# Routing products ahead of a second layer, weights' low parts later, and other places for the streamed tiles, in an attention and mixture-of-experts kernel

## The chip, the cores and the metric

The kernel runs on one core of a Trainium2 chip. The metric is the time of one execution on the device, in microseconds (us); it is the median of several runs. The engines are TensorE (PE in the rows; PEld is its weight load), VectorE (DVE), ScalarE (ACT), GpSimd (POOL) and SyncE (SP), which issues most of the DMAs.

## The reference

The first half is attention without a softmax: for each of 8 batches and 8 heads, the 64x64 product of keys and values over 576 positions is applied to the queries, and each row of 64 is divided by its root mean square and multiplied by g_norm. The second half sends each of the 4608 tokens (512 features) through one of 16 experts:

```
kv = np.einsum('bhsd,bhse->bhde', k, v)
out = np.einsum('bhsd,bhde->bhse', q, kv)
out = out / np.sqrt(np.mean(out * out, axis=-1, keepdims=True) + 1e-06) * g_norm
...
g_logits = x @ w_group                      # the group of 4 with the largest logit
e_logits = xg @ w_expert[g]                 # in it, the expert of 4 with the largest logit
h = np.maximum(xg[mask_e] @ w1[g, e], 0.0)  # 512 -> 1024
ye = h @ w2[g, e]                           # 1024 -> 512
out[tok_idx] = combined[:, None] * ye       # combined: the two softmax weights
```

## The kernel before

**Attention and routing (0 to about 128 us).** The 36 blocks of 128 tokens form six groups (`GS`). For each group the kernel computes the attention rows, stores them in a table in HBM (`scr`), and routes them: logits, the expert of each token, and its rank among the tokens of that expert. Which instruction stands where is decided by a planner: each piece of work is a `step` with an engine, an assumed duration, a rank and the steps it needs, and `give_out` hands them out in order of assumed time and rank. While the last groups are still routed, the expert that has most tokens early (the early expert, region 0) is already computed for 256 tokens: `early_products`, with float32 weights (`wr`), first layer into `h`, second layer into `l2` (`l_...` in the order's rows).

**The last routing products.** At the end, `slots` (one matmul per block) places the token numbers by expert and rank; `slt` is their sum so far. `eps` gives the experts' order by size, and from it `eidx`, the list of experts that the weight loads need. `gps` gives the token numbers of each expert in that order; VectorE turns it into the indices `gall`, which the gathers on POOL's queue need.

**The hand-over (about 128 to 159 us).** The early expert's second 128 tokens pass the second layer (`left`, two halves; `CUT` chunks of the second half run before the transposes of the third block's rows `xs`, the rest behind them). Its third block (`xr`, scaled to `xs`) then passes both layers in float32. Beside this the first streamed region is prepared: gather its rows (`xg`), scale them, store them to HBM (`xd`), load them back as `xq`, transpose them on VectorE (`xt`), split them into a high and a low part (`xh`, `xl`), and split the expert's weights in the same way (`whi`, `wlo`, by ScalarE and VectorE).

**The streamed regions (159 to 558 us).** The 15 other experts follow in order of size. Region r has `CAPS[r]` columns, one per token. Every product is a sum of three streamed matmuls in a reduced float32 format (fp32r): high x high, low x high and high x low. In the first layer each of 8 hidden chunks takes 4 x 3 matmuls (`ps`), in the second each of 4 output chunks 8 x 3 (`psy`): 192 matmuls of `CAPS[r]` columns a region. The weights are the stationary operand, the tokens (`xh`, `xl`, then `hh`, `hl`) are streamed. In the last region the second layer turns this round. While a region is computed, the next one is gathered, loaded, transposed and split, and its weights are loaded and split.

**Where tiles lie.** A pool gives tiles their places one behind the other. In the built program the weights (`w8`) begin at byte 27,008 of a partition plus whole multiples of 8,192, `xh` at 180,704, and `xl`, `hh`, `hl` whole multiples of 512 bytes behind `xh`; the float32 rows `xT` begin at 125,312 and `hT` at 127,360. A chunk of a streamed tile is 384 columns of 4 bytes, 1,536 bytes, so all chunks have the same place modulo 512.

Of the kernel before, what the change touches and what calls it, by code (L numbers as in the profile page):

```python
# [9 lines left out]
F32 = mybir.dt.float32  # L10
F32R = mybir.dt.float32r
# [3 lines left out]
ALU = mybir.AluOpType  # L15
# [5 lines left out]

CAPS = [384, 364, 354, 330, 326, 312, 302, 300, 292, 290, 284, 274, 268, 264, 260, 256]

# [30 lines left out]
MOVED = list(range(1, 15))  # L54
CUT = 5

@with_exitstack
def tile_linattn_moe(ctx: ExitStack, tc: tile.TileContext, qm, qt, k, v, router, w1, w2, out):
    nc = tc.nc
    P = 128  # L60
    B, H, S, D = BATCH, HEADS, SEQ, HEAD_DIM
# [15 lines left out]
    KC = DM // P  # L77
# [12 lines left out]
    ovt = tc.dram_tile([NBLK, 4], F32, name="ovt")  # L90

    cp = ctx.enter_context(tc.tile_pool(name="cp", bufs=1))
    big = ctx.enter_context(tc.tile_pool(name="big", bufs=BIG))

# [147 lines left out]

    def split_piece(w, p, turned=False):
        for x, hi, lo in quarter(w, p, turned):
            nc.scalar.copy(out=hi, in_=x)  # L245
            nc.vector.tensor_tensor(out=lo, in0=x, in1=hi.bitcast(F32), op=ALU.subtract)  # L246

# [88 lines left out]
    with ExitStack() as ph:  # L336
# [92 lines left out]
        def get(*key):  # L429
            return done.get(key)  # L430
# [199 lines left out]
        def route(g):  # L630
# [175 lines left out]
            def f():  # L806
                eng.tensor_tensor(
                    out=tl([1, NE, 6], "slot", BF16, bufs=1), in0=v["oh3"].unsqueeze(3).to_broadcast([P, nt, NE, 6]),
                    in1=v["jv"].rearrange("p t a j -> p t (a j)").unsqueeze(2).to_broadcast([P, nt, NE, 6]),
                    op=ALU.mult)  # L810
            sj = do(e, nt * 96, [sj, get("slots", g - 1)], f)

# [111 lines left out]
            if last:  # L924
                def f():
                    v["eps"] = ps_k.tile([P, 512], F32, name="eps", tag="psk")
                    nc.tensor.matmul(v["eps"][0:2, 0:3 * NE], lhsT=evec[0:NS, :], rhs=v["pmx"][0:NS, :], start=True,
                                     stop=True)
                x = do("PE", 0, [perm, done["ek", B - 1]], f, us=0.05)

                def f():
                    nc.vector.tensor_copy(out=eidx, in_=v["eps"][0:1, 0:3 * NE].rearrange("p (r j) -> p r j", j=3)[
                        :, :, 0])
                x = do("D", 16, [x], f)


                def f():
                    v["gps"] = ps_r.tile([P, 512], F32, name="gps", tag="psr")
                    nc.tensor.matmul(v["gps"][:, 0:3 * NE], lhsT=st["slt"][0:NS, :], rhs=v["pmx"][0:NS, :], start=True,
                                     stop=True)  # L940
                s = do("PE", 0, [s, x], f, us=0.1)

                def f():
                    nc.vector.tensor_scalar(out=gall[:, 0:3 * NE], in0=v["gps"][:, 0:3 * NE],
                                            scalar1=-1.0, scalar2=float(DUMMY), op0=ALU.mult, op1=ALU.add)
                done["gidx_last"] = do("D", 48, [s], f)
# [123 lines left out]
        def early_products(wt):  # L1070
# [34 lines left out]
            for j in range(1):  # L1105
                for hf in range(2):
                    def f(j=j, hf=hf):
                        t["l2", j, hf] = ps_e.tile([P, 512], F32, name="l2", tag="pse")
                        whole2(t["l2", j, hf][:, 0:DM // 2], t["h"][:, :, j * P:(j + 1) * P], st["ws"][2 + hf])
                    s = step("PE", 3.5, r0 + RANK["l2"] + 0.1 * (2 * j + hf), [free.pop(0), wt[2 + hf]] + hs, f)  # L1110

# [25 lines left out]
    with ExitStack() as ph:  # L1137
# [92 lines left out]
        def gather(r):  # L1230
            xg = mp.tile([P, 3, RW], F32, name="xg", bufs=1)
            for j, _ in blocks(CAPS[r]):
                st["gather"] = gather_rows(xg[:, j], P, gidx[:, r, j:j + 1])
            return xg
# [20 lines left out]

        def parts_x():
            return [mp.tile([P, KC, 384], F32R, name=nm, bufs=1) for nm in ("xh", "xl")]

# [70 lines left out]
        w1n, w2n, load_next = weight_loads(eidx[0:1, 1:2], mp)  # L1329
        for i in range(2):  # L1330
            load_next(i)
        nxt = gather(1)
# [11 lines left out]
        for p in range(2):  # L1344
            split_piece(w1n, p)
        keep_left(0)
        for j, _ in blocks(CAPS[1]):
            scale_rows(nc.vector, nxt[:, j])
        put_x(1, nxt)
        scale_rows(nc.vector, xr, xs)  # L1350
        xq, xt = get_x(1)
        for i in range(2, 4):
# [8 lines left out]
        scatter_rows(st["ys"][:, 1, :], P, gidx0[:, 1:2])  # L1361
        for p in range(2, 4):
            split_piece(w1n, p)

        for hf in range(2):
# [3 lines left out]
            nc.scalar.activation(out=hT[:, 4 * hf:4 * hf + 4], in_=ps.rearrange("p (f t) -> p f t", f=4), func=AF.Relu)  # L1369
        cur = parts_x()  # L1370
        for c in range(KC):
            turn_x(1, xq, xt, c)
        for c in range(KC):
            split_x(1, cur, xt, c)
        yo = mp.tile([P, DM], F32, name="yo", bufs=2)
        for hf in range(2):
# [13 lines left out]
        for r in range(1, NE):  # L1390
            cap = CAPS[r]
            xh, xl = cur
            hh = mp.tile([P, FC, 384], F32R, name="hh", bufs=1)
            hl = mp.tile([P, FC, 384], F32R, name="hl", tag="hl", bufs=1)
            if nxt:
# [32 lines left out]
            nw1a, nw2a, load_a = weight_loads(eidx[0:1, r + 2:r + 3], mp if r % 2 else None) if nxt2 else (None, None, None)  # L1428
            cur = parts_x() if nxt else None

# [139 lines left out]
```

## Time and profile before

| | us |
|---|---|
| runs: median (lowest to highest of 3) | 567.9 (567.41 to 568.88) |
| the profiled execution | 565.66 |
| its span, first to last instruction | 564.0 |
| TensorE busy | 543.9 |
| first streamed matmul / end of the last region's | 158.58 / 557.65 |

All rows are of the one profiled execution. The time of the profiled execution is its span and 1.66 us around it. Matmuls overlap: each is listed with a duration of about 300 ns, but the next one starts after 120 to 170 ns, so the spacing of their starts is what counts, not their durations. A float32 matmul appears as two entries in the counts. "issue" in the chain of waits is time in which the engine waited for nothing that the profile shows.

### The profile page before, as it was taken

What the parts mean: (1) busy time and instruction counts of PE and PEld (TensorE: products, weight loads), DVE (VectorE), ACT (ScalarE), POOL (GpSimd) and SP (SyncE); (2) the same over time, 40 slices, a digit from 0 to 9 for tenths busy, and PEclk for the clock granted to TensorE, in tenths of its full rate; (3) what the DMA queues carried; (4) which work ended last, traced back from release to release, by engine and by line L of the source; (5) the groups of instructions that cost most, each with busy time, mean ns of one, the idle gap of its engine ahead of it and who ended that gap; (6) DMA issues with size and microseconds to landing.
All of it is one profiled execution on the core that took longest, in us unless ns stands there. A gap on an engine that the chain in (4) does not pass through costs nothing.

```text
span 564.0 us, 11522 instructions
## 1 busy us (share of the span) xinstructions
PE 543.9 (96%) x4323; PEld 522.6 (93%) x4323; DVE 378.1 (67%) x782; ACT 267.1 (47%) x530; POOL 209.3 (37%) x278
## 2 busy tenths in 40 slices
PE   8999978699899999999999999999999999999995
PEld 3899868588899999999999999999999999999995
DVE  4247888773456796776767676777767686868750
ACT  0377754622444443544444544454546455546540
POOL 5024342144352342533453524344525334433121
PEclk9999998899999999999999999999999999999998
DMA  8999999486889999999998999999999999989940
GB/s 286 388 407 388 370 355 405 126 316 229 281 318 299 283 311 261 274 307 283 309 293 288 281 291 261 320 278 332 313 300 294 292 309 315 319 254 331 271 144 34
DMA packets 78890, 165.21 MB, mean 293 GB/s; under 512 B 8084, under 2 KB 47332, under 8 KB 67824
## 3 DMA queue, kind: packets, MB, share of 16 engines
q1 hardware_dynamic: 70862, 142.29, 78.7%
q0 software_dynamic: 7824, 22.11, 13.1%
q8 instruction: 35, 0.57, 0.4%
q10 hardware_dynamic: 146, 0.04, 0.1%
q14 instruction: 23, 0.19, 0.1%
HBM read 126.38 MB, written 38.55 MB: 292 GB/s over the span
## 4 chain that ended last, share of the span: by engine, by line
PE 69%; DMA 19%; issue 5%; DVE 2%; SPq 2%; ACT 2%; POOL 1%; POOLq 0%; DVEq 0%; ACTq 0%
PE ps L311 8%; PE ps L315 8%; PE ps L310 8%; DMA wr<-in_w_dram 8%; PE psy L311 8%; PE psy L310 8%; PE psy L315 8%; PE ops L515 5%; PE kps L477 3%; PE l L299 3%; PE warm L371 3%; DMA yd<-yq 2%; DMA xd<-xg 2%; DMA xq<-xd 2%; DMA ktail<-in_k_dram 2%
## 5 line engine op out<-in xcount | busy, mean ns | idle before, releaser
L246 DVE TENSOR_TENSOR wlo<-wr,whi 128x1024 fp32r<-128x1024 f32 (+1 forms) x176 | 156.6, 917 | 22.6 <-ACT whi L245 19.1
L311 PE MATMUL ps<-xl,whi 128*128 128x364 f32 (+14 forms) x480 | 144.5, 301 | 0.0
L315 PE MATMUL ps<-xh,wlo 128*128 128x364 f32 (+14 forms) x480 | 144.4, 301 | 0.0
L310 PE MATMUL ps<-xh,whi 128*128 128x364 f32 (+14 forms) x480 | 144.4, 301 | 0.0
L311 PE MATMUL psy<-hl,whi 128*128 128x364 f32 (+13 forms) x448 | 135.5, 302 | 0.0
L315 PE MATMUL psy<-hh,wlo 128*128 128x364 f32 (+13 forms) x448 | 135.4, 302 | 0.0
L310 PE MATMUL psy<-hh,whi 128*128 128x364 f32 (+13 forms) x448 | 135.2, 302 | 0.0
L245 ACT CAST whi<-wr 128x1024 fp32r<-128x1024 f32 (+1 forms) x176 | 128.2, 769 | 1.9 <-DMA wr<-in_w_dram 1.9
L284 ACT ACTIVATE hh<-ps 128x364 fp32r<-128x364 f32 (+14 forms) x120 | 50.4, 420 | 146.8 <-PE ps L315 142.4
L285 DVE SCALAR_TENSOR_TENSOR hl<-ps,hh 128x364 fp32r<-128x364 f32 (+14 forms) x120 | 55.8, 465 | 56.9 <-ACT hh L284 55.2
L310 PEld LDWEIGHTS ps<-xh,whi 128*128 128x128 f32 x480 | 90.8, 189 | 0.0
L315 PEld LDWEIGHTS ps<-xh,wlo 128*128 128x128 f32 x480 | 90.7, 189 | 0.0
L311 PEld LDWEIGHTS ps<-xl,whi 128*128 128x128 f32 x480 | 90.5, 189 | 0.0
L252 POOL DMA_INDIRECT xg<-scr,gall x44 | 52.6, 1196 | 96.2 <-DMA xd<-xg 81.2
L280 POOL TENSOR_TENSOR xg<-xg 128x256 f32<-128x256 f32 x82 | 60.2, 762 | 74.5 <-DMA xg<-scr,gall 74.4
L256 POOL DMA_INDIRECT out_dram<-yo,gall x45 | 51.8, 1150 | 92.8 <-DMA yo<-yd 75.9
L310 PEld LDWEIGHTS psy<-hh,whi 128*128 128x128 f32 x448 | 84.7, 189 | 0.0
L315 PEld LDWEIGHTS psy<-hh,wlo 128*128 128x128 f32 x448 | 84.7, 189 | 0.0
L311 PEld LDWEIGHTS psy<-hl,whi 128*128 128x128 f32 x448 | 84.5, 189 | 0.0
L1262 ACT ACTIVATE xh<-xt,rw 128x364 fp32r<-128x364 f32 (+14 forms) x60 | 32.3, 543 | 48.5 <-DVE xt L1253 45.5
L1315 DVE STREAM_TRANSPOSE yq<-psy 128x320 f32<-128x320 f32 (+3 forms) x56 | 28.5, 510 | 29.9 <-PE psy L315 27.6
L515 PE MATMUL ops<-kvx,m_q 128*128 128x168 f32 x256 | 42.0, 312 | 0.6 <-ACT xr L466 0.6
(250 smaller groups left out, 588.7 us busy)
## 6 DMA issues: line engine op xcount, KB each, us to landing
wr<-in_w_dram SPq DMA_DIRECT2D x64, 1024.0 KB
scr<-xo SPq DMA_DIRECT2D x36, 256.0 KB
m_q<-in_qm_dram SPq DMA_DIRECT2D x8, 1024.0 KB
xd<-xg SPq DMA_DIRECT2D x32, 256.0 KB
m_k<-in_k_dram SPq DMA_DIRECT2D x7, 1024.0 KB
m_v<-in_v_dram SPq DMA_DIRECT2D x7, 1024.0 KB
yo<-yd SPq DMA_DIRECT2D x28, 256.0 KB
xq<-xd SPq DMA_DIRECT2D x20, 160.0 KB
```

Source lines behind the costliest of these rows:

```text
L245: nc.scalar.copy(out=hi, in_=x)
L246: nc.vector.tensor_tensor(out=lo, in0=x, in1=hi.bitcast(F32), op=ALU.subtract)
L252: return nc.gpsimd.indirect_dma_start(out=xg[0:rows, 0:RW], out_offset=None, in_=src, in_offset=bass.IndirectOffsetOnAxis(ap=idx[0:rows, : ...
L256: sc = nc.gpsimd.indirect_dma_start(out=out, out_offset=bass.IndirectOffsetOnAxis(ap=idx[0:rows, :], axis=0), in_=yo[0:rows, :], in_offset ...
L280: d = eng.tensor_tensor(out=out_[:, hs], in0=x[:, hs], in1=factors(xg)[:, h], op=ALU.mult)
L284: nc.scalar.activation(out=hh, in_=ps, func=AF.Relu)
L285: nc.vector.scalar_tensor_tensor(out=hl, in0=ps, scalar=0.0, in1=hh.bitcast(F32), op0=ALU.max, op1=ALU.subtract)
L310: nc.tensor.matmul(ps, lhsT=stat_h(c), rhs=mov_h(c), start=(c == 0), stop=False)
L311: nc.tensor.matmul(ps, lhsT=stat_h(c), rhs=mov_l(c), start=False, stop=False)
L315: nc.tensor.matmul(ps, lhsT=stat_l(d), rhs=mov_h(d), start=False, stop=(d == n - 1))
L515: nc.tensor.matmul(o, lhsT=raw["q", b].rearrange("p j f -> p (j f)")[:, (pr * NJ + j) * P:(pr * NJ + j + 1) * P], rhs=kvx[b % 4][:, pr], s ...
L1262: nc.scalar.activation(out=xh, in_=x, func=AF.Copy, scale=g2[:, 0:1])
```

## The change

1. The second layer of the early expert (`l2`) now needs the step `done["last"]`, the last routing product `gps`; the planner can no longer put half of it ahead.
2. In the last group the product `slot` is computed on VectorE and no more on POOL.
3. The first streamed region's weights: the second half is loaded behind the stores of `xd`; the low parts of the first half are computed behind the scaling of the rows, and the second half is split behind `xh` and `xl`. `CUT` is 4 and no more 5.
4. Two regions get more columns: 326 becomes 330, 290 becomes 292.
5. Places: an unused tile of 8 floats ahead of all others moves everything by 32 bytes; `xg` is 24 floats (96 bytes) longer, so all that lies behind it, the streamed tiles among it, moves by 128 bytes; and a table `BEGIN` lets a region's streamed tiles begin at column 0, 8, 16 or 40 of the 384.

```
-CAPS = [384, 364, 354, 330, 326, 312, 302, 300, 292, 290, 284, 274, 268, 264, 260, 256]
+CAPS = [384, 364, 354, 330, 330, 312, 302, 300, 292, 292, 284, 274, 268, 264, 260, 256]
+BEGIN = [0, 16, 16, 0, 0, 0, 0, 0, 40, 40, 8, 0, 40, 0, 16, 0]
-CUT = 5
+CUT = 4
...
+    cp.tile([P, 8], F32, name="gap")
...
-    def split_piece(w, p, turned=False):
+    def split_piece(w, p, turned=False, high=True, low=True):
         for x, hi, lo in quarter(w, p, turned):
-            nc.scalar.copy(out=hi, in_=x)
-            nc.vector.tensor_tensor(out=lo, in0=x, in1=hi.bitcast(F32), op=ALU.subtract)
+            if high:
+                nc.scalar.copy(out=hi, in_=x)
+            if low:
+                nc.vector.tensor_tensor(out=lo, in0=x, in1=hi.bitcast(F32), op=ALU.subtract)
...
-                eng.tensor_tensor(
+                (nc.vector if last else eng).tensor_tensor(
                     out=tl([1, NE, 6], "slot", BF16, bufs=1), ...
-            sj = do(e, nt * 96, [sj, get("slots", g - 1)], f)
+            sj = do("D" if last else e, nt * 96, [sj, get("slots", g - 1)], f)
...
-                s = do("PE", 0, [s, x], f, us=0.1)
+                s = done["last"] = do("PE", 0, [s, x], f, us=0.1)
...
-                    s = step("PE", 3.5, r0 + RANK["l2"] + 0.1 * (2 * j + hf), [free.pop(0), wt[2 + hf]] + hs, f)
+                    s = step("PE", 3.5, r0 + RANK["l2"] + 0.1 * (2 * j + hf), [free.pop(0), wt[2 + hf], done["last"]] + hs, f)
...
-            xg = mp.tile([P, 3, RW], F32, name="xg", bufs=1)
+            xg = mp.tile([P, 3 * RW + 24], F32, name="xg", bufs=1)[:, 0:3 * RW].rearrange("p (j f) -> p j f", j=3)
...
-        def parts_x():
-            return [mp.tile([P, KC, 384], F32R, name=nm, bufs=1) for nm in ("xh", "xl")]
+        def streamed(r, nm, n=KC):
+            return mp.tile([P, n, 384], F32R, name=nm, bufs=1)[:, :, BEGIN[r]:BEGIN[r] + CAPS[r]]
+        def parts_x(r):
+            return [streamed(r, nm) for nm in ("xh", "xl")]
...
-        for i in range(2):
-            load_next(i)
+        load_next(0)
...
         for p in range(2):
-            split_piece(w1n, p)
+            split_piece(w1n, p, low=False)
...
         scale_rows(nc.vector, xr, xs)
+        for p in range(2):
+            split_piece(w1n, p, high=False)
+        load_next(1)
         xq, xt = get_x(1)
...
-        for p in range(2, 4):
-            split_piece(w1n, p)
...
         for c in range(KC):
             split_x(1, cur, xt, c)
+        for p in range(2, 4):
+            split_piece(w1n, p)
...
-            hh = mp.tile([P, FC, 384], F32R, name="hh", bufs=1)
-            hl = mp.tile([P, FC, 384], F32R, name="hl", tag="hl", bufs=1)
+            hh, hl = (streamed(r, nm, FC) for nm in ("hh", "hl"))
```

On TensorE at the hand-over, from the experts' order (`eps`) to the first float32 layer of the third block (`ps<-xT`), before; `l_...` are the two halves of the early expert's second layer, `left` those of its second 128 tokens:

```order
L927 MATMUL eps<-permx,evec 2x48
L303 MATMUL l_1890<-wr_1673,h 128x256 x8
L939 LDWEIGHTS slt
L939 MATMUL gps<-permx,slt 128x48
L303 MATMUL l_1901<-wr_1708,h 128x256 x8
L303 MATMUL left<-wr_1673,h 128x256 x8
L303 MATMUL left<-wr_1708,h 128x256 x5
L1357 MATMUL ps<-ident,xs 128x128 x4
L303 MATMUL left<-wr_1708,h 128x256 x3
```

The same place on TensorE after the change:

```order
L933 MATMUL eps<-permx,evec 2x48
L309 MATMUL left<-wr_1674,h 128x256
L945 LDWEIGHTS slt
L945 MATMUL gps<-permx,slt 128x48
L309 MATMUL l_1893<-wr_1674,h 128x256 x8
L309 MATMUL l_1903<-wr_1709,h 128x256 x8
L309 MATMUL left<-wr_1674,h 128x256 x7
L309 MATMUL left<-wr_1709,h 128x256 x4
L1369 MATMUL ps<-ident,xs 128x128 x4
L309 MATMUL left<-wr_1709,h 128x256 x4
```

`gps` stands ahead of both halves of the second layer; one chunk of `left` stands between it and `eps`, and one chunk of the other half has moved behind the transposes.

On VectorE at the same place, from the experts' order to the first streamed region, before:

```order
L1020 SCALAR_TENSOR_TENSOR permx<-r_98,kown,jmask 128x48
L900 TENSOR_TENSOR slt<-slots,slt 96x128
L932 CAST eidx<-eps 1x16
L944 TENSOR_SCALAR gall<-gps 128x48
L246 TENSOR_TENSOR wlo<-wr_1944,whi 128x4x256 x2
L280 TENSOR_TENSOR xg<-xg 128x256 x6
L280 TENSOR_TENSOR xs<-xr 128x2x4x32 x2
L246 TENSOR_TENSOR wlo<-wr_1946,whi 128x4x256 x2
L1253 STREAM_TRANSPOSE xt<-xq 128x384 x4
L1263 SCALAR_TENSOR_TENSOR xl<-xt,rw,xh 128x364 x4
```

And after:

```order
L813 TENSOR_TENSOR slot<-ohb,jv 128x384
L1026 SCALAR_TENSOR_TENSOR permx<-r_99,kown,jmask 128x48
L906 TENSOR_TENSOR slt<-slots,slt 96x128
L938 CAST eidx<-eps 1x16
L950 TENSOR_SCALAR gall<-gps 128x48
L286 TENSOR_TENSOR xg<-xg 128x256 x6
L286 TENSOR_TENSOR xs<-xr 128x2x4x32 x2
L252 TENSOR_TENSOR wlo<-wr_1945,whi 128x4x256 x2
L1260 STREAM_TRANSPOSE xt<-xq 128x384 x4
L1273 SCALAR_TENSOR_TENSOR xl<-xt,rw,xh 128x364 x4
L252 TENSOR_TENSOR wlo<-wr_1988,whi 128x4x256 x2
```

The first weights' low parts (`wlo`) have moved behind the scaling of the gathered rows, those of the second half behind `xl`, and `slot` is new here.

On SP's queue of DMAs, from the first streamed region's weights on, before:

```order
L207 TENSOR_LOAD eidx
L212 DMA wr_1944<-in_w_dram 128x2048
L212 DMA wr_1946<-in_w_dram 128x2048
L1242 DMA xd_59<-xg 128x512 x3
L1248 DMA xq<-xd_59 32x12x128 x4
```

And after:

```order
L211 TENSOR_LOAD eidx
L216 DMA wr_1945<-in_w_dram 128x2048
L1249 DMA xd_59<-xg 128x512 x3
L216 DMA wr_1988<-in_w_dram 128x2048
L1255 DMA xq<-xd_59 32x12x128 x4
```

The load of the second half of the weights has moved behind the stores of the rows and stands directly ahead of their loading back.

## Rows read from the trace of the kernel before

**Rows 1.** The page's first section: busy time, share of the span, instructions.

```profile
PE 543.9 (96%) x4323; PEld 522.6 (93%) x4323; DVE 378.1 (67%) x782; ACT 267.1 (47%) x530; POOL 209.3 (37%) x278
```

**Rows 2.** TensorE by region: stretch, length, busy, (matmuls), granted clock, DMA share, GB/s.

```profile
158.58:190.86 32.28, 32.28 (x194) 1.00 1.00 307
190.86:222.85 31.99, 31.99 (x194) 1.00 1.01 285
222.85:252.29 29.44, 29.44 (x193) 1.00 0.95 289
252.29:281.42 29.13, 29.13 (x195) 1.00 1.01 290
281.42:309.15 27.73, 27.73 (x194) 1.00 0.93 292
309.15:336.03 26.88, 26.88 (x195) 1.00 1.02 294
336.03:362.90 26.87, 26.87 (x194) 1.00 0.99 293
362.90:388.31 25.41, 25.41 (x195) 1.00 1.01 300
388.31:414.54 26.23, 26.23 (x194) 1.00 1.02 320
414.54:440.15 25.61, 25.61 (x195) 1.00 0.98 288
440.15:464.68 24.53, 24.53 (x195) 1.00 0.97 281
464.68:488.15 23.47, 23.47 (x195) 1.00 0.98 298
488.15:511.50 23.35, 23.35 (x194) 1.00 0.91 294
511.50:534.56 23.06, 23.06 (x195) 1.00 0.99 305
534.56:557.65 23.09, 23.06 (x194) 1.00 0.36 118
```

**Rows 3.** The chain of waits at the hand-over: start us, us, engine, tile, line.

```profile
135.55 5.61 PE left L303 x26
141.16 1.79 issue
...
144.88 7.14 PE ps L299 x64
152.02 6.91 PE ps L303 x32
```

**Rows 4.** Timeline of all engines there: start us, us, engine, line, operation, [idle before <-releaser].

```profile
128.25 0.29 DVE L900 TENSOR_TENSOR slt<-slots,slt 96x128 bf16<-96x128 f32 x1 [0.97 <-PE slots L892]
...
131.81 0.19 PE L939 MATMUL gps<-permx,slt 96*128 96x48 bf16 x1
...
133.03 1.06 POOL L252 DMA_INDIRECT xg<-scr,gall  x1 [5.83 <-DVE gall L944]
...
135.16 2.36 DVE L246 TENSOR_TENSOR wlo<-wr,whi 128x1024 fp32r<-128x1024 f32 x2 [2.90 <-ACT whi L245]
...
137.50 1.17 POOL L252 DMA_INDIRECT xr<-scr,gall  x1 [0.30 <-issue]
...
142.08 0.76 DVE L280 TENSOR_TENSOR xs<-xr 128x256 f32<-128x256 f32 x2 [1.48 <-DMA xr<-scr,gall]
...
154.13 2.08 DVE L1263 SCALAR_TENSOR_TENSOR xl<-xt,rw,xh 128x364 fp32r<-128x364 f32 x4
```

**Rows 5.** Timeline of VectorE in the last regions, the same columns.

```profile
504.04 0.84 DVE L1253 STREAM_TRANSPOSE xt<-xq 128x288 f32<-128x288 f32 x2 [1.44 <-DMA xq<-xd]
...
511.06 0.45 DVE L1263 SCALAR_TENSOR_TENSOR xl<-xt,rw,xh 128x260 fp32r<-128x260 f32 x1
...
534.19 0.44 DVE L1263 SCALAR_TENSOR_TENSOR xl<-xt,rw,xh 128x256 fp32r<-128x256 f32 x1
```

More of the change, by code (lines that the diff above doesn't have):

```diff
@@ L1369, in tile_linattn_moe @@
             nc.scalar.activation(out=hT[:, 4 * hf:4 * hf + 4], in_=ps.rearrange("p (f t) -> p f t", f=4), func=AF.Relu)
-        cur = parts_x()
+        cur = parts_x(1)
         for c in range(KC):
@@ L1428, in tile_linattn_moe @@
             nw1a, nw2a, load_a = weight_loads(eidx[0:1, r + 2:r + 3], mp if r % 2 else None) if nxt2 else (None, None, None)
-            cur = parts_x() if nxt else None
+            cur = parts_x(r + 1) if nxt else None
             def side(n, total, after):
```

## The prediction

> **What bounds the kernel now.** I read the page's first section, then the busy times by stretch, then the chain of waits and the timeline around the step from the routing to the experts, and last VectorE's timeline near the end. The page says that TensorE is busy for 543.9 of 564.0 us and no other engine for more than 378.1 [rows 1]. The busy times, cut at the first matmul of each of the regions 1 to 15, show where: from 158.58 to 557.65 us TensorE never rests, at a granted clock of 1.00 (the level of 2.4 GHz) [rows 2]. A region is 192 streamed matmuls (8 hidden chunks of 12, then 4 output chunks of 24; the counts of 193 to 195 include neighbours that reach over the cut), so each row divided by 192 is the spacing of that region's matmuls. Those 399 us move only if the spacing moves. Ahead of them stands one gap: the chain runs through TensorE from 128 us on, with a hole of 1.79 us at 141.16 [rows 3]. So I ask two things: what becomes of the gap, and what of the spacing.
>
> **The spacing, as the rows have it.** 268 columns: 23.47 us / 192 = 122.2 ns. 292 columns: 25.41 / 192 = 132.3 ns. The step between them, 10.1 ns for 24 columns, is 0.42 ns a column. I draw the line through these two, 122.2 + 0.42 x (columns - 268), and measure every other region against it: 364: +5.5 ns; 354: +8.2; 330: +5.0; 326: +5.1; 312: +3.7; 302: +3.5; 300: +4.2; 290: +5.1; 284: +4.5; 274: +3.1; 264: +1.1; 260: +1.3; 256: +3.0 [rows 2]. No region lies below the line. That this is not only a matter of width is seen at 290 against 292: two columns fewer cost 26.23 instead of 25.41 us. So a matmul loses up to 8 ns to something that depends on how the stream lies, and it does so at one single layout: before the change the streams of all regions begin 96 bytes (modulo 512) away from the weights.
>
> **The gap at 141 us.** What ends it is a chain that starts late: the last routing product gps runs at 131.81, behind a half of the early expert's second layer, although its operands were there at 128.5; gall follows, then POOL's first gather at 133.03, its fourth, xr, at 137.50, the scaling of xr at 142.08, and the transposes at 142.95 [rows 3, 4]. Now gps stands right behind eps, with one chunk of a later product between them. That chunk is two of the 26 entries that take 5.61 us [rows 3], 0.43 us, about as long as VectorE needs for slt and eidx; I price what is left of the wait at 0 to 0.3 us and take 0. Behind gps on TensorE stand both halves of the second layer; they start 0.6 us later and are waited for only by ScalarE's copies. gps at 128.8 instead of 131.8 brings the four gathers to 130.0 to 134.5, xr (4.6 us from issue to the scaling in these rows) to 139.1, and the scaled rows to 139.9. TensorE, its work unchanged in sum, comes to the transposes at 141 or sooner (one chunk less stands ahead of them, since CUT is 4). The gap is then covered by 1 us: -1.8 us. Bounds: 0 if the gathers are held by something else, -1.8 if all goes, since no more than the gap is there.
>
> What the same edits move beside it. The low parts of the first weights (2.36 us of VectorE at 135.16 [rows 4]) go behind the scaling; they are needed at the first streamed matmul, now at 156.8, and have 14 us of cover; without it they would cost their 2.36 us. The slot product goes from POOL to VectorE ahead of permx, at less than 1 us; eps waits for TensorE's earlier products anyway, so 0, and up to 0.5 us if not. The second weight half is issued behind three stores of xd and ahead of the loads of xq on SP's queue: a MB, some 3.5 us at the 281 to 320 GB/s of regions 1 to 14 [rows 2], now stands before xq. But xd leaves about 3 us earlier, and the last xl of region 1 ended at 156.21 against a start at 158.58 [rows 2, 4], so it comes out about even: 0, with 1 us as the price if xq is later. Its own split goes behind xh; it is needed 96 / 2 = 48 matmuls, 8 us, into the region: 0.
>
> **The columns and the places.** 290 becomes 292 and 326 becomes 330. The pads move the weights by 32 bytes and the streams by 128; with the first columns the distance between stream and weights becomes 192 bytes (modulo 512) for eight regions (330 twice, 312, 302, 300, 274, 264, 256), 256 for three (364, 354, 260), 352 for both regions of 292 and for 268, 224 for 284. Modulo 128 that is 64, 0, and the old 96.
>
> - The four regions that keep 96 modulo 128: I leave 292, 268 and 284 at their rows; the one that was 290 takes the row of 292: 25.41 - 26.23 = -0.8 us.
> - The eleven others: no row shows their distances. The bounds from the rows: all on the line, 5.5 + 8.2 + 5.0 + 3.4 + 3.7 + 3.5 + 4.2 + 3.1 + 1.1 + 1.3 + 3.0 = 42.0 ns (the 3.4 is 326's 151.7 against the line at 330), x 192 = -8.1 us; all as far off as 354 is, 11 x 8.2 - 42.0 = 48 ns, x 192 = +9.3 us. The row that is nearest in layout: the unstreamed float32 products of the hand-over, whose operands lie a multiple of 512 bytes apart, as near to 256 or 64 as this trace has it. Their 64 entries of 128 columns take 7.14 us, 111.6 ns, and 32 entries of 256 columns 6.91 us, 216 ns [rows 3]: 104.4 ns for 128 columns more, 7.2 ns beside the columns, nothing lost that grows with them. They read at half the rate, so I trust them for the sign alone, and take half of the way to the line: -4.0 us.
>
> Sum: -1.8 - 0.8 - 4.0 = -6.6 us. The profiled execution took 565.66 us (564.0 of span), 2.2 below the median of 567.9, so I take the sum from the median: 561.3, said as 561.
>
> **A rule that speaks against it.** The spacing depends on more than width [rows 2]. The Trainium skill, SBUF — State Buffer, section "Who interferes with whom", gives TensorE two independent read ports, one for the moving operand and one for weight loads, and says that it never waits on anyone. By that rule the distance between the two can't matter, and the eleven regions keep their rows; no row here has a second distance to hold against it. That is the first rival below, whose time is worked out from rows.
>
> **Rivals.**
> 1. The places change nothing. For it: one layout only is in the trace, and at it the losses differ by width alone. Against it: 290 against 292, where nothing but the end of the stream differs. Then 330 takes 29.44 instead of 29.13 us (+0.3), 292 its -0.8, the gap -1.8: -2.3 us, 565.6.
> 2. Slower: the weights begin 32 bytes off their old place, and each weight load now meets its stream for longer. All 15 regions would then lie as the three worst rows do, (8.2 + 5.5 + 5.1) / 3 = 6.3 ns above the line. At their present places they would sum, with the new widths, to 42.0 + 4.5 = 46.5 ns; so 15 x 6.3 - 46.5 = 48 ns, x 192 = +9.2, less 2.6: 574.5. It decides from a mean of 2.6 / 0.192 / 15 = 0.9 ns a matmul. For it speaks that 11 of 15 regions show 3 ns and more already; against it, the float32 rows.
> 3. The data comes too late for a faster TensorE. In the last regions the tokens are barely in time: region 14 starts at 511.50 and its last xl ends at 511.51, region 15 at 534.56 and 534.63, where the fourth chunk is read nine matmuls, 1.1 us, later; VectorE waited 1.44 us for xq at 504.04 [rows 2, 5], and the DMA share of regions 1 to 14 is 0.91 to 1.02 [rows 2]. If the DMA does not follow, what TensorE gains beyond that 1.1 us is lost in region 14: about 566.5. Against it: the weights are not waited for, and up to region 13 there is more room.
>
> **How the numbers follow.** The forecast gets 0.55, with 557 to 563 of its own (from 567.9 - 10.7 with all on the line, to a third of the way). Rival 1 gets 0.20, rival 2 0.15, rival 3 0.10. The range reaches from 555 (a layout may beat the line by 1 ns a matmul in the eleven regions, 2.1 us) over rivals 1 and 3 to 569, where rival 2 is only begun; outside it are most of rival 2 and some of the forecast's tail. A measurement of this kernel can tell about 0.3%, 1.7 us. Faster: nearly all of the forecast, two thirds of rival 1, half of rival 3: 0.73. Within: the rest of these two and the mild part of rival 2: 0.14. Slower: 0.13.
>
> **What would show it.** In the profile after: gps at about 129 and no hole in the chain ahead of the transposes; first streamed matmul at 156.8; 25.4 us for each region of 292 columns and 23.5 for 268; 364, 354, 330, 302 and 300 shorter by 0.3 to 0.8 us each; no idle time of TensorE before regions 14 and 15. I am wrong on the gap if xr still lands after TensorE is free; on the spacing if the eleven regions stand at their rows (rival 1) or above them (rival 2); and rival 3 shows as idle time ahead of xh in the late regions.

## The result, and the profile after

The changed kernel took 562.29 us (median of 20 executions, 557.72 to 571.17), the kernel before 568.96 (20 executions) on the same chip: a ratio of 0.9853, 95% interval 0.9827 to 0.9878. Put on the chip a second time, the same kernel took 563.31 us (8 executions, 560.37 to 567.04) against 567.49, a ratio of 0.9918 (0.9882 to 0.9953). A ratio leaves out executions more than 1.5% above the kernel's fastest one, seven of the changed kernel's 20 here (566.64 to 571.17 us, perhaps the stalled ones of the third group of experiments below, of which none here has a trace) and none the second time. With all of them the medians divide to 0.9883 and 0.9926. So the kernel is faster, by 0.7 to 1.5% as one counts, and the first 20 executions spread over 13 us.

The profiled execution took 561.67 us, 4.0 less than that of before: span 560.0 against 564.0. The page's first section, in answer to [rows 1]:

```profile
PE 539.9 (96%) x4315; PEld 519.6 (93%) x4323; DVE 379.7 (68%) x783; ACT 266.7 (48%) x530; POOL 214.0 (38%) x277
```

TensorE by region, cut as in [rows 2] (stretch, length, busy, matmuls, granted clock, DMA share, GB/s; some regions left out):

```profile
158.16:190.35 32.19, 32.19 (x194) 1.00 1.03 311
190.35:221.08 30.73, 30.73 (x194) 1.00 1.04 307
221.08:250.84 29.76, 29.76 (x194) 1.00 0.93 285
250.84:280.60 29.76, 29.76 (x194) 1.00 0.99 285
...
334.46:360.71 26.25, 26.25 (x195) 1.00 0.97 299
...
386.10:411.49 25.39, 25.39 (x195) 1.00 0.94 301
411.49:436.57 25.08, 25.08 (x195) 1.00 0.97 288
...
507.43:530.63 23.20, 23.06 (x194) 1.00 0.96 312
530.63:553.13 22.50, 22.50 (x193) 1.00 0.38 122
```

Against [rows 2]: the region of 354 columns is shorter by 1.26 us, 300 by 0.62, 290 as 292 by 0.84, 284 by 0.53; 330 is longer by 0.32, and 326 as 330 by 0.63. From the first streamed matmul to the last one's start it is 394.97 us instead of 398.76. The row of 507.43 is the only one with a hole: 23.20 long, 23.06 busy.

The chain at the hand-over (start us, us, engine, tile, line), in answer to [rows 3]:

```profile
129.78 0.11 PE eps L933
129.89 0.63 PE left L309 x2
130.52 0.03 PE gps L945
130.54 7.00 PE l L309 x32
137.54 4.75 PE left L309 x22
142.29 0.44 PE ps L1369 x4
```

The timeline there, in answer to [rows 4]:

```profile
130.36 0.19 PE L945 MATMUL gps<-permx,slt 96*128 96x48 bf16 x1
...
131.07 1.04 POOL L258 DMA_INDIRECT xg<-scr,gall  x1 [3.18 <-DVE gall L950]
...
134.97 0.95 POOL L258 DMA_INDIRECT xr<-scr,gall  x1 [0.30 <-issue]
...
138.76 0.76 DVE L286 TENSOR_TENSOR xs<-xr 128x256 f32<-128x256 f32 x2
...
156.85 2.08 DVE L1273 SCALAR_TENSOR_TENSOR xl<-xt,rw,xh 128x364 fp32r<-128x364 f32 x4
```

gps now stands 0.65 us behind eps, no "issue" stands in the chain, and from eps to the first streamed matmul it is 28.45 us; it was 30.44. The first streamed matmul comes only 0.42 us earlier (158.16 against 158.58), because eps itself came 1.57 us later in this execution; over the profiles of all kernels below it lies between 128.1 and 132.0 us, early and late ones with and without the change. So the 4.0 us are +1.57 of that, -1.99 at the hand-over, -3.79 in the streaming, +0.23 behind it. The last xl of regions 14 and 15, in answer to [rows 5], with region 14 starting at 507.43 and region 15 at 530.63:

```profile
507.86 0.45 DVE L1273 SCALAR_TENSOR_TENSOR xl<-xt,rw,xh 128x260 fp32r<-128x260 f32 x1
...
530.21 0.44 DVE L1273 SCALAR_TENSOR_TENSOR xl<-xt,rw,xh 128x256 fp32r<-128x256 f32 x1
```

The first ends 0.88 us after its region has begun, the second 0.02 us. TensorE reads the last xl nine matmuls, 1.07 us, into the region, and waited for neither. The hole in the row of 507.43 lies later, ahead of the matmul at 514.86, and weights stand behind it: in ScalarE's, VectorE's and TensorE's timeline the cast whi of region 14's own second layer waits 1.65 us for its weights' DMA, wlo waits for whi, hl (514.39 to 515.15, two of them) stands behind wlo, and the matmul waits for the first hl:

```profile
512.52 1.14 ACT L250 CAST whi<-wr 128x512 fp32r<-128x512 f32 x2 [1.65 <-DMA wr<-in_w_dram]
513.18 1.29 DVE L252 TENSOR_TENSOR wlo<-wr,whi 128x512 fp32r<-128x512 f32 x2 [1.50 <-ACT whi L250]
514.86 0.39 PE L316 MATMUL ps<-xh,whi 128*128 128x260 f32 x1
```

### The profile page after: what moved, and what is told of

Same layout as the page of the kernel before. It is cut to its first block, busy times and chain, and to the rows that moved or that the text cites. A ratio compares the mean times of both kernels' runs of the same rounds, so it can differ in the third digit from the quotient of the medians.

```text
span 560.0 us, 11511 instructions
## 1 busy us (share of the span) xinstructions
PE 539.9 (96%) x4315; PEld 519.6 (93%) x4323; DVE 379.7 (68%) x783; ACT 266.7 (48%) x530; POOL 214.0 (38%) x277
## 4 chain that ended last, share of the span: by engine, by line
PE 61%; DMA 28%; issue 4%; DVE 2%; ACT 1%; POOL 1%; SPq 1%; POOLq 0%; DVEq 0%; ACTq 0%
DMA wr<-in_w_dram 11%; PE ps L317 8%; PE ps L316 8%; PE ps L321 8%; PE psy L317 7%; PE psy L316 7%; PE psy L321 7%; PE ops L521 4%; DMA yd<-yq 4%; PE l L305 3%; DMA m_q<-in_qm_dram 3%; DMA m_k<-in_k_dram 3%; PE kps L483 2%; DMA ktail<-in_k_dram 2%; DMA m_v<-in_v_dram 2%
## 5 line engine op out<-in xcount | busy, mean ns | idle before, releaser
L316 PE MATMUL ps<-xh,whi 128*128 128x330 f32 (+12 forms) x480 | 144.0, 300 | 0.1
L317 PE MATMUL ps<-xl,whi 128*128 128x330 f32 (+12 forms) x480 | 143.9, 300 | 0.0
L321 PE MATMUL ps<-xh,wlo 128*128 128x330 f32 (+12 forms) x480 | 143.7, 299 | 0.0
L317 PE MATMUL psy<-hl,whi 128*128 128x330 f32 (+11 forms) x448 | 134.8, 301 | 0.0
L316 PE MATMUL psy<-hh,whi 128*128 128x330 f32 (+11 forms) x448 | 134.7, 301 | 0.0
L321 PE MATMUL psy<-hh,wlo 128*128 128x330 f32 (+11 forms) x448 | 134.6, 301 | 0.0
L290 ACT ACTIVATE hh<-ps 128x330 fp32r<-128x330 f32 (+12 forms) x120 | 50.2, 420 | 140.2 <-PE ps L321 130.9
L262 POOL DMA_INDIRECT out_dram<-yo,gall x45 | 57.6, 1281 | 103.7 <-DMA yo<-yd 83.4
L291 DVE SCALAR_TENSOR_TENSOR hl<-ps,hh 128x330 fp32r<-128x330 f32 (+12 forms) x120 | 55.6, 465 | 49.6 <-ACT hh L290 44.9
L1272 ACT ACTIVATE xh<-xt,rw 128x330 fp32r<-128x330 f32 (+12 forms) x60 | 32.3, 543 | 50.8 <-DVE xt L1260 50.8
```

Of the source, the lines that this page charges most:

```text
L262: sc = nc.gpsimd.indirect_dma_start(out=out, out_offset=bass.IndirectOffsetOnAxis(ap=idx[0:rows, :], axis=0), in_=yo[0:rows, :], in_offset ...
L290: nc.scalar.activation(out=hh, in_=ps, func=AF.Relu)
L291: nc.vector.scalar_tensor_tensor(out=hl, in0=ps, scalar=0.0, in1=hh.bitcast(F32), op0=ALU.max, op1=ALU.subtract)
L316: nc.tensor.matmul(ps, lhsT=stat_h(c), rhs=mov_h(c), start=(c == 0), stop=False)
L317: nc.tensor.matmul(ps, lhsT=stat_h(c), rhs=mov_l(c), start=False, stop=False)
L321: nc.tensor.matmul(ps, lhsT=stat_l(d), rhs=mov_h(d), start=False, stop=(d == n - 1))
```

## Experiments

**1. Is it the distance?** Three theories: the stream's own place counts, the weights' own place, or the distance between them. First kernel: the kernel before with the pad of 32 bytes alone, which moves weights and streams together. Second: with the longer xg alone, which moves the streams by 96 bytes.

```
+    cp.tile([P, 8], F32, name="gap")                  # both32
```

```
-            xg = mp.tile([P, 3, RW], F32, name="xg", bufs=1)                # stream96
+            xg = mp.tile([P, 3 * RW + 24], F32, ...)[:, 0:3 * RW].rearrange(...)
```

> The kernel before with the unused tile of 8 floats alone: weights and streams both move by 32 bytes, their distance stays 96 (modulo 512). Theory D (the distance between the weights and the streamed tile sets the spacing, by width): every region as before, 399.1 us for regions 1 to 15, 153.3 ns at 330 columns, 166.6 at 354, 136.6 at 290. Rival S (the streamed tile's own place sets it): the streams now begin at 0 instead of 480 modulo 512, so several widths move by 2 ns or more. Rival W (the weights' own place sets it, 384 to 416): the widths move towards those after the change, 155.0 at 330, 137.8 at 302, 136.8 at 300.

> The kernel before with the row tile xg 96 bytes longer alone: the weights stay, the streams move by 96 bytes, the distance is 192 (modulo 512), as in the eight regions of the changed kernel that begin at column 0. Theory D: those widths have the changed kernel's spacing, 155.0 ns at 330, 142.7 at 312, 137.8 at 302, 136.8 at 300, 126.7 at 274, 120.1 at 264, 117.8 at 256. Rival W (the weights' own place): all as before, 153.3, 144.4, 140.0, 139.9, 127.8, 121.6, 120.1. Rival S: neither of the two rows.

Measured: 566.73 and 565.79 us, one execution each. The regions of 330 and 256 columns with both moved:

```profile
223.94:253.38 29.44, 29.44 (x194) 1.00 0.88 280
...
535.64:558.43 22.79, 22.79 (x193) 1.00 0.28 84
```

The regions of 364, 330, 292 and 256 columns with the stream moved against the weights:

```profile
161.39:194.01 32.62, 32.62 (x194) 1.00 1.00 312
...
226.00:254.61 28.61, 28.61 (x194) 1.00 0.90 287
...
363.49:389.73 26.24, 26.24 (x195) 1.00 0.99 309
...
535.77:557.42 21.65, 21.65 (x193) 1.00 0.30 92
```

The first pair is that of [rows 2] to 0.01 us (256 is cut here at the last matmul's start). In the second 364 got longer by 0.34, 330 shorter by 0.83, 292 longer by 0.83, 256 shorter by 1.14. So moving both by 32 bytes does nothing, a change of the distance does, and each width has its own answer. Five of the seven spacings that the theory of the distance gave came (312, 302, 300, 274 and 264 columns, to 0.1 ns); two did not: 330 columns ran at 149.0 ns instead of 155.0, and 256 at 113.4 instead of 117.8. The third group comes back to these.

**2. The two halves of the change.** The hand-over alone is the changed kernel with the places and the columns taken back; places alone is the kernel before with the pads, CAPS and BEGIN of the change.

```
-BEGIN = [0, 16, 16, 0, 0, 0, 0, 0, 40, 40, 8, 0, 40, 0, 16, 0]      # handover
+BEGIN = [0] * 16          # and CAPS, gap, xg as before
```

```
+BEGIN = [0, 16, 16, 0, 0, 0, 0, 0, 40, 40, 8, 0, 40, 0, 16, 0]      # places
 ...                       # and CAPS, gap, xg as after, all else as before
```

> The changed kernel with its places and columns undone: the hand-over edits alone (routing products first, low parts later). Theory: the first streamed matmul comes 2.0 us sooner after the last eps product (28.4 us instead of 30.4), regions 1 to 15 take 399.1 us as before, and the time falls by 1.8 us, 0.3%. Rival: the gain is lost because xq comes too late for region 1 (its last xl ended 0.8 us after the region's start in the changed kernel): 0.

> The kernel before with the places and columns of the change alone, hand-over as before. Theory: regions 1 to 15 take 395.3 us instead of 399.1, the gap of 1.8 us ahead of the transposes stays, and the time falls by 3.8 us, 0.7%. Rival: the 32 bytes also slow the float32 products of the attention (the last eps product stood 1.6 us later in the changed kernel's profile): then only 2.2 us, 0.4%.

The hand-over alone: 568.5 us, a ratio of 1.0021 (0.9992 to 1.0049), nothing gained where 1.8 us were expected. Its 28.45 us are there, but in region 1 TensorE has a new hole (the column in brackets is the idle time):

```profile
167.55 0.43 PE L315 MATMUL ps<-xh,whi 128*128 128x364 f32 x1 [2.81 <-DVE hl L290]
```

Places alone: 563.34 us, a ratio of 0.9904 (0.9871 to 0.9937). The gap of 1.81 us stays, the streaming takes 395.04 us, with three holes at the end of region 13 and in region 14, where VectorE is late (for the last of them, as in the first profile of the change, because the cast whi before it had waited, here 2.01 us, for its weights):

```profile
505.88 0.40 PE L313 MATMUL psy<-hh,whi 128*128 128x264 f32 x1 [0.30 <-DVE yq L1321]
...
511.28 0.39 PE L314 MATMUL ps<-xl,whi 128*128 128x260 f32 x1 [1.01 <-DVE xl L1269]
...
517.99 0.39 PE L313 MATMUL ps<-xh,whi 128*128 128x260 f32 x1 [0.50 <-DVE hl L288]
```

Both regions of 330 columns take 28.59 us in this run, where the changed kernel, with the same widths, pads and first columns, had 29.76. That is the riddle of the next runs.

**3. The changed kernel again, and the hole in region 1.** Once unaltered, and once with both halves of the first weight fetched at the start, as before.

```
-        load_next(0)                                  # early
+        for i in range(2):
+            load_next(i)
...
-        load_next(1)
```

> The changed kernel a second time, nothing altered; one core, other execution. In its first profile the two regions of 330 columns had a matmul every 155.0 ns, while two other kernels with the same widths and the same distance between weights and stream had 149.0. Theory R (the rhythm at 330 columns has two states, chosen by how a region is entered, so one and the same kernel can show either): this profile may show 149 in one or both regions, the streaming then being 1.2 us shorter for each, and the times of single executions lie several us apart, as they did the first time (557.7 to 571.2 us). Theory P (the rhythm is fixed by what is laid where in SBUF, and this kernel differs from the two others in some place not looked at): 155.0 in both regions again, every other spacing within 0.3 ns of the first profile. Under both, the time against the kernel before is 0.983 to 0.992 of it, and from the last product of the early expert to the first streamed matmul it takes 28.4 to 31.3 us (28.45 if the second weight's last piece lands in time, up to 2.8 us more in region 1 if it doesn't).

> The changed kernel with one thing put back: both halves of the first weight are fetched at the start, ahead of the gather for region 1, as in the kernel before; the routing product stays ahead of the second layer. Theory Q (in the run with the hand-over alone the gain of 2.0 us was given back because the second half was fetched 10 us later, which pushed the last quarter of the second weight to 165 us, behind which ScalarE's evacuations queued): the packets of the first weight are done by 142 us as before, no TensorE gap over 0.3 us in region 1, the 28.45 us from the early expert's last product to the first streamed matmul stays, and the time is 1 to 2 us under that of the changed kernel on the same chip. Rival T (the late fetch has nothing to do with it, the loads of the second weight wait for their buffers): a gap of 1 to 3 us in region 1 in this kernel too, or the last piece of the second weight as late as before, and the time equal to the changed kernel's within 0.3%. Rival U: with the second half fetched early the gathers behind it on the same queue land later, the product that waits for them starts later, and the 28.45 us grow to 29.5 or more; time equal or up to 1 us longer.

The second profile of the unaltered kernel, regions 1, 3, 4 and 15:

```profile
158.11:195.55 37.44, 33.98 (x194) 0.95 0.93 281
...
226.28:254.86 28.58, 28.58 (x193) 1.00 0.87 276
254.86:283.45 28.59, 28.59 (x195) 1.00 1.05 296
...
533.56:555.23 21.67, 21.67 (x194) 1.00 0.38 117
```

330 columns take 28.58 and 28.59 us, not 29.76, and 256 21.67, not 22.50: one kernel, two rhythms. In the first profile the starts at 330 columns follow each other after 153, 157, 152, 158 ns, over and over; in this one after 145, 149, 153. The regions of 364 and 354 ahead of them run alike in both, to 0.1 ns a matmul. Together the two rhythms are 3.2 us apart. And region 1 took 37.44 us, 33.98 of it busy. The chain of waits there (some pieces left out):

```profile
143.42 10.29 DMA xg<-scr,gall
...
153.78 1.20 POOL xg L286 x2
...
157.40 8.00 DMA out_dram<-yos,gall
...
165.47 0.63 ACT whi L250
...
166.12 1.29 DVE wlo L252 x2
167.41 0.46 DVE hl L291
...
167.91 0.43 PE ps L316
```

Read from the bottom: the matmul at 167.91 waited for VectorE's hl to free a PSUM buffer; hl stood behind wlo, wlo waited for ScalarE's cast whi, and whi behind a DMA that has nothing to do with weights: the scatter of the early expert's rows from yos, 8.00 us long. In the built program whi of the second weight's first half has the buffer that yos had; the pool hands it on as soon as yos has been read, and its last reader is that scatter. It goes out only at 157.40, since GpSimd's queue has the scaling of region 2's gathered rows ahead of it (153.78 is its second block), which waits for gathers of 10.29 us. In the kernel before, the same buffer goes to a half of region 2's second weight, fetched in region 1 and split in region 2. The profile of the first execution has a wait of ScalarE at the same cast, 1.70 us that TensorE did not feel. Its row names no releaser, so that it is the same wait is likely and not shown:

```profile
161.76 1.14 ACT L250 CAST whi<-wr 128x512 fp32r<-128x512 f32 x2 [1.70 <-issue]
```

TensorE in stretches of 2 us in the second profile, with the granted clock behind its busy time, shows why region 1 took 5.25 us more than in the first profile (37.44 against 32.19), and not only the 3.46 us that it stood still:

```profile
164.00:166.00 2.00, 0.45 (x3) 1.00 1.00 413
166.00:168.00 2.00, 0.09 (x1) 1.00 1.02 360
168.00:170.00 2.00, 2.00 (x9) 0.72 1.07 221
170.00:172.00 2.00, 2.00 (x8) 0.50 1.19 212
172.00:174.00 2.00, 2.00 (x13) 0.93 1.25 217
```

After the hole it is at 0.50 (the level of 1.2 GHz) for some 3 us, with no wait left: 8 matmuls touch a stretch of 2 us, where 14 do at 1.00 (162 to 164 us).

Fetching early did not help: 567.9 us, a ratio of 0.9991 (0.9968 to 1.0013), 4.6 us above the unaltered kernel in the same comparison. The last packets of the second weight landed by 157 us, and yet the hole was 4.01 us. (Its profile, of 563.95 us, is one of its fastest executions; what the others add is not shown.) VectorE in that run:

```profile
166.79 1.29 DVE L252 TENSOR_TENSOR wlo<-wr,whi 128x512 fp32r<-128x512 f32 x2 [7.79 <-issue]
```

And GpSimd:

```profile
159.65 1.03 POOL L262 DMA_INDIRECT out_dram<-yos,gall  x1 [0.17 <-ACT whi L250]
```

Here the buffer of yos went to wlo, and wlo waited until 166.79 for the scatter of 159.65. Theory Q falls, and so do T, which blamed the loads' wait for their buffers, and U: from eps to the first streamed matmul it is 28.59 us, not 29.5.

**4. Other distances.** The first column at 8, and at 16, in all regions.

```
+BEGIN = [0] + [8] * 15        # all8
+BEGIN = [0] + [16] * 15       # all16
```

> The changed kernel with the first column at 8 in each of the fifteen regions: the stream lies 224 bytes from the weights modulo the row, against 96 in the kernel before and 192, 256 or 352 by region in the changed one. Theory D1 (what counts is the distance modulo 128 bytes): each width shows the spacing it had at a distance of 96, so 284 columns 133.4 ns, 364 167.2, 354 166.6, 330 153.3, 256 119.3, 292 132.3, 268 122.2. Theory D2 (modulo 256 bytes or more): 284 stays at 130.6 as in the changed kernel, and at least three other widths differ from their value at 96 by over 1 ns. No theory gives the single values under D2; the streaming is 393 to 402 us.

> The changed kernel with the first column at 16 in each of the fifteen regions: a distance of 256 bytes everywhere, where the changed kernel has it for 364, 354 and 260 columns only. Theory D (distance and width set the spacing): these three stay at 166.7, 160.0 and 118.7 ns. If the distance modulo 64 bytes is what counts, 312, 302, 300, 274, 264 and 256 also stay as they are at 192 (142.7, 137.8, 136.7, 126.7, 120.2, 117.8), and the regions at 352 change from 132.3 (292) and 122.2 (268). If the table in the changed kernel holds the best place for each width, none of these gets shorter by over 0.5 ns and the streaming is longer than 395 us.

Spacing in ns, from the starts of the matmuls, by width and by distance in bytes modulo 512 (96: the kernel before; 192: the stream moved by 96 bytes, the changed kernel for eight regions; 224 and 256: first column at 8 and at 16; 352: the changed kernel; where two values stand, both were seen at one layout):

| columns | 96 | 192 | 224 | 256 | 352 |
|---|---|---|---|---|---|
| 364 | 167.2 | 168.9 | 166.7 | 166.6 | |
| 354 | 166.6 or 163.3 | 166.6 | 161.7 | 160.0 | |
| 330 | 153.3 | 149.0 or 155.0 | 153.3 | 153.3 | |
| 312 | 144.4 | 142.7 | 143.4 | 142.9 | |
| 302 | 140.0 | 137.8 | 140.0 | 137.8 | |
| 300 | 140.0 | 136.7 | 138.5 | 140.0 | |
| 292 | 132.3 | 136.7 | 133.4 | 133.4 | 132.3 |
| 284 | 133.4 | 133.3 | 130.7 | 133.3 | |
| 274 | 127.8 | 126.7 | 127.5 | 129.9 | |
| 268 | 122.2 | 124.4 | 124.6 | 124.5 | 122.2 |
| 264 | 121.7 | 120.2 | 120.0 | 121.4 | |
| 260 | 120.1 | 120.0 | 119.9 | 118.7 | |
| 256 | 119.3 | 113.4 or 117.8 | 117.5 | 119.9 | |

D1 (modulo 128) falls: 284 differs by 2.7 ns between 96 and 224, 354 by 4.9, 268 by 2.4. A count modulo 64 falls too: 300 differs by 3.3 ns between 192 and 256. 96 and 352, 256 bytes apart, agree for both widths that have them; no other pair 256 bytes apart was measured. But for the slower rhythms at 330 and 256, the places of the change are the best of what was measured, or within 0.2 ns of it. Both kernels had the hole in region 1 (4.94 and 4.71 us); it is in their single times, 572.37 and 571.34 us.

**5. The scatter ahead of the scalings.** In the changed kernel, in the hand-over alone, and, as a control, in the kernel before.

```
         nxt = gather(2)
-        scale(2, nxt)
...
         scatter_rows(st["ys"][:, 1, :], P, gidx0[:, 1:2])
+        scale(2, nxt)
```

> The changed kernel with one move: the scatter of the early expert's second half (out_dram from yos, on GpSimd's queue) stands ahead of the three scalings of region 2's gathered rows instead of behind them. Theory Y (the changed order gives the buffer of yos to the high part of the second weight's first half, region 1; its cast on ScalarE, or the subtraction on VectorE, waits until the scatter of yos has landed, at 165.4 us in one profile; the evacuations wait behind it and TensorE stands for 2.8 to 5 us, and then runs some 3 us at the halved clock): the scatter goes out at 145 to 147 us and has landed by 156, no TensorE gap over 0.3 us in region 1, that region's excess over its own rhythm under 0.5 us (5.44, 5.96 and up to 7.2 us in the runs with the stall), and a median 2 to 5 us under that of the changed kernel, 0.980 to 0.987 of the kernel before. Rival Z (the cast waits for its weights, which land late, and the scatter only lands at the same time): the scatter lands early and the gap of 2 us or more in region 1 stays, the ratio stays at 0.985 to 0.992.

> The hand-over alone (places and columns as before, which had a ratio of 1.002) with the scatter of yos ahead of the scalings of region 2. Theory Y: the gap of 2.81 us in region 1 goes, the 28.45 us from the early expert's last product to the first streamed matmul stays, the spacings are those of the kernel before, and the time is 1.5 to 2.5 us under the kernel before: a ratio of 0.9955 to 0.9975, which is the first part of the change by itself. Rival Z: the gap stays and the ratio is 1.000 to 1.004.

> A control: the kernel before with the same move of the scatter. There the buffer of yos goes to a part of region 2's second weight, whose fetch is issued in region 1 and which is needed 25 us later. Theory Y: nothing changes, no gap in region 1 with or without the move, a single time of 565 to 570 us, the streaming 398.3 to 399.3 us. If an earlier scatter helps or hurts by itself (through the DMA engines that it shares with the gathers), the first streamed matmul moves by over 0.3 us against the last product of the early expert (30.44 us).

The changed kernel with the move: 560.21 us (557.45 to 562.44), a ratio of 0.9834 (0.9801 to 0.9868). The scatter goes out at 144.54, in GpSimd's timeline:

```profile
144.54 1.02 POOL L262 DMA_INDIRECT out_dram<-yos,gall  x1 [0.30 <-issue]
```

No hole is left in region 1, in the row of that region:

```profile
156.98:189.16 32.18, 32.18 (x195) 1.00 1.00 316
```

The hand-over alone with the move: 567.42 us, 0.9981 (0.9956 to 1.0006), against 1.0021 (0.9992 to 1.0049) without. The hole in region 1 is gone here too, but the expected 0.9955 to 0.9975 was missed, the interval still reaches over 1, and in its profile region 14 took 24.24 us against 23.06 [rows 2], with a hole of 0.91 us behind a cast whi that had waited 2.46 us for its weights. The control: 566.63 us, streaming 398.77 us, no hole with or without. Theory Y stands for the hole, and Z falls: of the profiles of the hand-over's order, five of the six with the late scatter have the hole (all but the first), and none of the three with the earlier one has it (these two and that of the sixth group). In time the move is not clear of the noise: its interval overlaps with that of the hand-over alone without it, and with the changed kernel's first one, though not with its second.

**6. What chooses the rhythm?** In the kernel with the earlier scatter, one short product ahead of the regions 3, 4 and 15, whose result the next one overwrites.

```
+                if f == 0 and r in (3, 4, 15):
+                    nc.tensor.matmul(ps[:, 0:64], lhsT=w1c[0][1][:, 0, 0:P], rhs=xh[:, 0, 0:64], start=True, stop=True)
```

> The changed kernel with the earlier scatter, and one short product of 64 columns ahead of the first streamed matmul of regions 3, 4 (330 columns) and 15 (256 columns); its result is overwritten by the product behind it. It costs under 0.5 us at each place. What is open: the same kernel has shown 330 columns at 155.0 and at 148.9 ns and 256 at 117.8 and at 113.4. Theory F (a region falls into one of two rhythms by the phase in which its first weight load meets the stream, and keeps it): the short product shifts that phase, so at least one of the three regions shows the other rhythm than in the run with the earlier scatter alone (155.0, 155.0, 117.8), and each that flips is 1.2 us (330) or 0.8 us (256) shorter; with all three the time is 1.5 to 3 us under 560.2 us. Rival G (the rhythm is set by something that lasts from region 1 on, whether TensorE had stood still there or not): 155.0, 155.0 and 117.8 in all three again, and the time is 0 to 1.5 us above that of the run with the earlier scatter alone.

The regions 3 and 15, cut ahead of the short product:

```profile
219.49:249.35 29.86, 29.86 (x195) 1.00 0.90 279
...
529.12:551.53 22.41, 22.10 (x194) 1.00 0.45 145
```

330 stays in the slow rhythm (29.76 and 0.10 for the product), in region 4 too; 256 runs at 113.2 ns a matmul, the fast one, with 0.67 us for the product and a wait. So a shift at the region's start does not decide 330, against theory F; 256 is the one region that F's wording allows and G's does not, but whether the product did it is not sure, since 256 changes by itself. The time, 562.47 us, 0.9917 (0.9889 to 0.9946), was in a comparison of its own above that of the kernel it was made from (0.9834, 0.9801 to 0.9868); its profiled execution, 560.02, was its fastest and shows no reason. What chooses the rhythm stays open.

## Why the prediction was right, and where it was not

- **The gap, -1.8 us: right in its mechanism.** gps right behind eps, four gathers earlier, the scaled rows done at 139.52, 2.6 us ahead of the transposes; 28.45 instead of 30.44 us, -1.99.
- **The moved weights, priced at 0: the step that failed.** The load of the first weight's second half ahead of xq ("it comes out about even: 0") and its later split ("8 us, into the region: 0") were priced by the data and the queues, but not by the buffers. The edits changed which tile takes over the buffer of yos, and with it who waits for a scatter that was free before: 3.1 us in the hand-over alone (region 1 took 35.37 us), 5.25 in the second profile of the changed kernel, 0 in the first. As a whole the hand-over gained nothing that the runs can tell from zero (1.0021, and 0.9981 with the scatter moved, both intervals reaching over 1). The price that the prediction named beside this step, 1 us if xq came late, was not what came: xq was late, and the four xl, done by 156.21 before [rows 4], ran until 158.93, 0.77 us into region 1, but TensorE reads the last of them nine matmuls later and did not wait.
- **290 as 292, -0.8: right**, 26.23 to 25.39.
- **Eleven regions half-way to the line, -4.0: right in sign, by luck in size.** Without the wait in region 14 the first profile has -2.8 us and the second -6.0, one on each side. The difference is the two rhythms, of which the prediction knew nothing. 354 came from 8.2 to 1.7 ns above the line, 300 from 4.2 to 1.1, 364 hardly moved (its 5.5 ns above the line were 4.6 by the starts of its matmuls, 167.2 ns, since its row has a slow first step in it); 330 is at 0.8 or 6.7, and 256 at 0.6 above or 3.8 below, where no region lay before.
- **Four regions stay, modulo 128: wrong for 284**, which gave 0.53 us; right for 292 and 268, whose distance is the old one modulo 256.
- **Rival 1 falls**, with the rule behind it: the Trainium skill, SBUF — State Buffer, "Who interferes with whom", has TensorE's two read ports independent and TensorE never waiting. Here 292 columns streamed against the same weights, moved by 96 bytes, take 26.24 us a region instead of 25.41; the measurement decides, though it does not say where in the path the two meet.
- **Rival 2 falls**: weights 32 bytes farther on cost nothing as long as the stream moves with them.
- **Rival 3 is there in small, and not as argued**: region 14, 22.79 us at its own spacing, took 23.20 in the first profile, 24.53 with the earlier scatter and 25.01 with places alone. Late tokens were a part of it only: TensorE stood for xl 0.51 us with the earlier scatter and 1.01 with places alone, and in all three for an hl behind weights that came late (0.14, 0.71 and 0.50 us). That the weights are not waited for, which the prediction held against this rival, was no longer so. (By its own terms, 567.9 less 1.1, its price comes to 566.8 and not to 566.5.)

The sum: places alone gave 0.9904, some 5.5 us, where 4.8 were forecast; the hand-over alone came out 1.2 us above instead of 1.8 below, which its interval (-0.5 to 2.8 us) does not tell from nothing. Together that is 4.3 us, about what the second comparison has (0.9918 is 4.7 us); the first has 6.7 between the medians, near the forecast's 6.6, which is luck: the gap's part did not come in the time, and the places gave more than their part. Which of the rhythms and holes its executions had is not known, since only one of them has a trace.

## What to carry to other kernels

When an edit moves where tiles of a pool are first used, list which tile now takes over each buffer and who reads that buffer last, the DMAs included: the wait shows up at an engine and at a time that have nothing to do with the edit. Profile one kernel twice before explaining a spacing. Where a weight load goes on beside a stream, the place of one against the other is worth a sweep for each width; here the two widths that were measured 256 bytes apart agreed, and no rule in the width was found.

## What the runs showed of the hardware

- The spacing of streamed matmuls depends on the distance between weights and stream, by up to 6.6 ns of 167 (354 columns, 96 or 256 bytes), and did not change when both moved by 32 bytes (398.78 us of streaming against 398.76).
- At one layout there can be two rhythms, kept over a whole region: 149.0 and 155.0 ns at 330 columns, 113.4 and 117.8 at 256, 166.6 and 163.3 at 354 (the hand-over alone with the earlier scatter had the latter).
- A hole of 3.46 us was followed by some 3 us at a granted clock of 0.50, so it cost 5.25 us in all.
- A scatter of 128 rows took 8.00 us, from its issue to the cast that waited for it, beside other DMAs (a DMA share of 0.89 in that time).
